# Pooled attention and two MLPs on one core: a scheduler that hands out PSUM banks when they come free, an earlier release of a conversion's source block, and other DMA costs

## The chip, the core and the metric

The kernel runs on one core of a Trainium2 chip. The metric is the device time of one execution in microseconds (us). Five engines work side by side, each through its own queue in order: TensorE (PE, matmuls into the eight PSUM banks), ScalarE (ACT), VectorE (DVE), GpSimd (POOL) and SyncE (SP, which issues all DMAs here).

## The reference

```python
q_pool = q.reshape(B, H, S // 2, 2, D).mean(axis=3)          # 4 batches, 8 heads, 1152 rows, 64 wide
scores = (1 / sqrt(D)) * q_pool @ k.T                         # 576 x 1152 a head
attn   = exp(scores - max) / (sum(exp) + 1e-9)
x = (attn @ v) as [2304 tokens, 512]
h = x @ moe_w_in;  x = max(0.01 * h, h) @ moe_w_out           # 512 -> 2048 -> 512
h = x @ moe2_w_in; out = where(h > 0, h, exp(min(h, 0)) - 1) @ moe2_w_out
```

The four weight matrices reach the kernel as float64, and the kernel turns their bits into float32 itself. Each float32 operand is split in a high and a low part in a rounded format, and products take two or three matmuls.

## The kernel before

Work is recorded as operations with an engine, a cost in ns, a rank and a function; `Program.schedule` then plays a clock forward and starts, on each idle engine, the open operation of least rank, and `emit` writes the instructions in the order of the starts. What the engines run is that order, each in its own queue; on the chip an instruction waits only for its data and its buffers. So costs, latencies and buffer rules in the scheduler move instructions and change none.

There are 16 attention pairs (four batches, four pairs of heads) of nine score tiles each. A score tile is three blocks of 384 keys, each a PSUM bank: matmuls (L486), a maximum on DVE (L491), the exponential on ACT (L497), transposes (L509) of its result into PSUM, a high part on ACT and a low part on DVE (L298, L304), then the product with v (L530). Beside the attention of batches 1 to 3 run the two MLPs of the batch before; those of batch 3 come last and alone ("wide"). An MLP has 16 steps; in each, 24 matmuls (L672) fill two banks, ACT and DVE empty them (L683, L685 in the first MLP; L688, L691, L693 in the second), and after each four steps `down` forms eight more banks (L710), which ACT or DVE adds up (L720, L723). `store` transposes the result (L744), copies it on ACT into one of two `cr` buffers (L750) and sends it out.

PSUM before: tags with a fixed number of banks, taken in turn in the order in which operations were recorded: `s` 3 for scores, `t` 2 for transposes, `o` 1 for the product with v, `h` 2 for the MLPs. In the first four pairs transposes also take `h` banks; a wide MLP takes `h`, `t` and `s` banks in turn.

`convert` fetches a block of float64 into `cr` (L327, two buffers), reads its high words on ACT into `cm` (L330), its low words on ACT in place (L332), shifts on DVE (L334) into `ct`, adds on POOL (L337) reading `cr`, and merges on DVE into the weight tile `wr` (L339). Each block is converted once, stored to DRAM and read back for the later batches.

An operation of class `Port` is a DVE operation that shares SBUF ports with POOL by the scheduler's account; it never plays one beside a POOL operation. POOL gives way to an open `Port` operation that DVE will soon be free for (`HOLD` 500 ns) if that one's rank is below POOL's rank plus `HELD`.

Of the kernel before, what the change touches and what calls it, by code (L numbers as in the profile page):

```python
# [22 lines left out]
class Buf:  # L23


    def __init__(self, make, prev=None, before=None):
        self.make, self.prev, self.before = make, prev, before
        self.tile, self.first = None, None
        self.writers, self.readers = [], []

# [3 lines left out]
    @property  # L34
    def ap(self):
        if self.tile is None:
            self.tile = self.make()
        return self.tile


class Program:

# [7 lines left out]
    HELD = 5  # L50
    LATENCY = {"PE": 200, "SP": 2500, "DVE": 130, "DVE POOL": 200, "ACT": 155, "ACT POOL": 170, "POOL": 150,
               "PE PE": 5}

    def __init__(self):
        self.ops, self.tags = [], {}
# [7 lines left out]
    def add(self, engine, cost, rank, fn, w=(), r=()):  # L63

        me = len(self.ops)
        deps, starts, frees = set(), set(), []
# [8 lines left out]
        for x in w:  # L75
            b, part = x if isinstance(x, tuple) else (x, None)
            deps.update(hits(b.writers, part))
            deps.update(hits(b.readers, part))
            if b.first is None:
                b.first = me  # L80
            if b.prev is not None:
# [5 lines left out]
        self.ops.append((engine, cost, rank, fn, deps, starts, frees))  # L87

    def schedule(self):
# [3 lines left out]
        for i, (_, _, _, _, deps, starts, frees) in enumerate(ops):  # L93
# [9 lines left out]
            need[i] = len(d | starts)  # L103
        ready = [0.0] * n
# [10 lines left out]
        left = n  # L115
        while left:
# [4 lines left out]
            while again:  # L121
                again = False
                for e in sorted(idle, key=lambda e: e == "POOL"):
# [5 lines left out]
                    i = open_[e][0][1]  # L129
                    if e == "POOL":  # L130
                        if port > now:
                            continue
                        if idle["DVE"] <= now + self.HOLD and any(
                                isinstance(ops[o][1], Port) and r < ops[i][2] + self.HELD
                                for r, o in open_["DVE"]):
                            if idle["DVE"] > now:
                                heapq.heappush(times, idle["DVE"])
                                continue
                    if e == "DVE" and port > now and isinstance(ops[i][1], Port):
                        others = [x for x in open_[e] if not isinstance(ops[x[1]][1], Port)]  # L140
                        if not others:
                            continue
                        x = min(others)
                        open_[e].remove(x)
                        heapq.heapify(open_[e])
                        heapq.heappush(open_[e], (-1e9, x[1]))
                        i = x[1]
# [4 lines left out]
                    heapq.heappop(open_[e])  # L152
# [4 lines left out]
                    if e == "POOL" or isinstance(ops[i][1], Port):  # L157
                        port = end
                    again = True
                    for o, done in out[i]:  # L160
                        e2 = ops[o][0]
                        if not done:
                            t = now
                        elif e2 == "PE" and e not in ("PE", "SP"):
                            t = end + 200
                        else:
                            t = end + self.LATENCY.get(e + " " + e2, self.LATENCY[e])
                        ready[o] = max(ready[o], t)
                        need[o] -= 1
                        if not need[o]:  # L170
                            heapq.heappush(waiting[e2], (ready[o], o))
                            heapq.heappush(times, ready[o])
        return start

    def emit(self, tc):
        start = self.schedule()
        held, name = None, None
        for i in sorted(range(len(start)), key=lambda i: (start[i], i)):
            engine, cost, _, fn, deps, _, _ = self.ops[i]
# [11 lines left out]
def kernel(  # L191
# [54 lines left out]
    SBUFS = 3  # L246
    RAWB = 3
    EARLY = {'s': 'sss', 't': 'tthh'}
    T1B = 3
    HBUFS = 2  # L250
# [3 lines left out]
    TB = 2  # L254
# [27 lines left out]
    def bank(tag, shape, dt=F32, bufs=1):  # L282
        return prog.buf(tag, bufs, lambda: ps.tile(shape, dt, tag=tag, name=tag, bufs=bufs))
# [8 lines left out]
    def pool(n):  # L292
        return 140 + 2.12 * n

    def psplit(rank, h, l, hi, lo, src, n, w, r, w_l=None, fast=True, psum=False):
# [3 lines left out]
        else:  # L299
            prog.add("DVE", dve(n, fast), rank, lambda: V.tensor_copy(out=hi(), in_=src()), w=[w], r=r)  # L300
# [7 lines left out]
    def convert(rank, dst, src):  # L308

        for n in range(0, 512, CW):
            r = sb("cr", [128, CW, 2], U32, CB)
            t = sb("ct", [128, CW], U32, CB)
            g = sb("cm", [128, CW], F32, CB)

            def load(n=n, r=r):  # L320
# [8 lines left out]
            prog.add("SP", 60, rank - 1, load, w=[r])  # L329
            prog.add("ACT", act(CW, sbuf=True), rank, lambda r=r, g=g: A.activation(  # L330
                out=g.ap, in_=r[:, :, 1].bitcast(F32), func=ACTF.Copy, scale=REBIAS), w=[g], r=[(r, 1)])
            prog.add("ACT", act(CW, sbuf=True), rank, lambda r=r: A.activation(  # L332
                out=r[:, :, 0], in_=r[:, :, 0], func=ACTF.Copy, scale=2.0 ** -29), w=[(r, 0)], r=[(r, 0)])
            prog.add("DVE", dve(CW, True), rank, lambda g=g, t=t: V.tensor_scalar(  # L334
                out=t.ap, in0=g.ap.bitcast(U32), scalar1=3, scalar2=None,
                op0=ALU.logical_shift_left), w=[t], r=[g])
            prog.add("POOL", pool(CW), rank, lambda t=t, r=r: G.tensor_tensor(  # L337
                out=t.ap, in0=t.ap, in1=r[:, :, 0], op=ALU.add), w=[t], r=[t, (r, 0)])
            prog.add("DVE", dve(CW, port=True), rank, lambda n=n, t=t, g=g: V.scalar_tensor_tensor(  # L339
                out=dst[:, n:n + CW].bitcast(U32), in0=g.ap.bitcast(U32), scalar=0x80000000, in1=t.ap,  # L340
                op0=ALU.bitwise_and, op1=ALU.bitwise_or), w=[(dst, n)], r=[t, g])
# [3 lines left out]
    def load_w(rank, layer, w_in, w_out, f, mine):  # L345
# [4 lines left out]
        for i, r in enumerate(rs):  # L350
            if w_in.dtype == F32:
                view = (lambda r=r: r.ap.rearrange("p (c n) -> p c n", c=DC)) if i == 0 else lambda r=r: r.ap
                prog.add("SP", 60, rank - 1.5, lambda i=i, view=view: nc.sync.dma_start(
                    out=view(), in_=src[i]), w=[r])
            elif (layer, f, i) in kept:
                kp = kept[layer, f, i]
                prog.add("SP", 60, rank - 1.5, lambda r=r, kp=kp: nc.sync.dma_start(
                    out=r.ap, in_=kp.ap), w=[r], r=[kp])
            else:
                convert(rank - CLEAD, r, src[i])  # L360
                kp = kept[layer, f, i] = Buf(lambda i=i: dram.tile([128, 512], F32, name=f"w{layer}_{f}_{i}"))
                prog.add("SP", 60, rank, lambda r=r, kp=kp: nc.sync.dma_start(out=kp.ap, in_=r.ap), w=[kp], r=[r])
# [17 lines left out]
    def load(rank, key, tag, shape, pieces, bufs):  # L380
        t = sb(tag, shape, F32, bufs)
        for i, (to, src) in enumerate(pieces):
            prog.add("SP", 60, rank, lambda to=to, src=src: nc.sync.dma_start(out=to(t), in_=src), w=[(t, i)])
# [18 lines left out]
    def tr_r(rank, src, get, n):  # L402
# [6 lines left out]
        prog.add("PE", 70 * n, rank, go, w=[t], r=[src])  # L409
        return t  # L410

    def prep_k(rank, b, hp, j):
# [5 lines left out]
        for c in range(3):  # L418
            t = tr_r(rank, kn, lambda i, c=c: kn[:, 3 * c + i, :], 3)
# [18 lines left out]
    def prep_q(rank, b, hp, j):  # L438
        qn = q_split(rank, raw[b, hp, j, "q"], QT, "q")
        qT = sb("qT", [128, 2, QT, 128], F32R, KTB)  # L440
        for a in range(2):
            t = tr_r(rank, (qn, a), lambda i, a=a: qn[:, a, i, :], QT)
# [4 lines left out]
    def prep_rem(rank, b, hp):  # L447
        qn = q_split(rank, raw[b, hp, "x"], 1, "qx")
        t = tr_r(rank, qn, lambda i: qn[:, i, 0, :], 2)
# [13 lines left out]
    turns = {}  # L463
    BANKS = dict(s=SBUFS, t=TB, o=1, h=HBUFS)

    def pbank(use, dt=F32, shape=(128, 4, 128)):
        tags = (EARLY if first_window[0] else {}).get(use, use)
        n = turns[use] = turns.get(use, -1) + 1
        tag = tags[n % len(tags)]
        return bank(tag, list(shape), dt, BANKS[tag])  # L470
# [32 lines left out]
    def transpose_p(rank, p, dests):  # L503
        for c in ORDER:
# [8 lines left out]
            prog.add("PE", 3 * 108, rank, tr, w=[t], r=[(p, c)])  # L513
# [9 lines left out]
    def pv(rank, b, hp, j, pt, col0, n):  # L523
        o = pbank("o", F32, (128, 512))
        vn = prep[b, hp, j, "v"]

# [7 lines left out]
        for th in ORDER:  # L534
            prog.add("PE", 6 * (7 + 0.4375 * n), rank + PVLAG, lambda th=th: mm(th), w=[o], r=[vn, pt[th]])
        if (b, hp) not in xu:
            xu[b, hp] = sb("xu", [128, NQ], F32, XFB)
        x = xu[b, hp]
        hi, lo = slice(64 * j, 64 * j + 64), slice(64 - 64 * j, 128 - 64 * j)
        tm = sb("tm", [128, 5 * 64])  # L540
        prog.add("ACT", act(n), rank + PVLAG, lambda: A.activation(
# [87 lines left out]
    def mlp(at, span, b, layer, xin, w_in, w_out, tags):  # L629

        step = span / (FT + 1)
        turn = [0]

        def hbank():
            tag, bufs = tags[turn[0] % len(tags)]
            turn[0] += 1
            return bank(tag, [128, 512], F32, bufs)
# [3 lines left out]
        def mine(tag, shape, dt, bufs, other, more):  # L641

            seq = ((tag, bufs),) * bufs + (((other, more),) * more if len(tags) > HBUFS else ())
# [17 lines left out]
        def up(f):  # L661
# [4 lines left out]
            for hf in range(2):  # L666
                cols = slice(hf * HB, hf * HB + HB)
                h = hbank()

# [10 lines left out]
                t = mine("t1", [128, HB], F32, T1B, "raw", RAWB)  # L680
# [52 lines left out]
    def store(at, b, acc, tags):  # L733
        turn = 0
        for t in range(QT + 1):
            n = 128 if t < QT else RQ
            tag, bufs = tags[turn % len(tags)]
            turn += 1
            p = bank(tag, [128, 512], F32, bufs)
# [15 lines left out]
            prog.add("SP", 60, at, lambda o=o, n=n, rows=rows: nc.sync.dma_start(  # L755
# [56 lines left out]
```

## Time and profile before

| | |
|---|---|
| median of 3 runs | 1486.04 us (1485.85 to 1488.83) |
| the profiled execution | 1488.3 us, span 1486.5 us |
| PE busy | 1403.5 us, 94% of the span |
| ACT busy | 1058.6 us, 71% |
| DVE busy | 886.0 us, 60% |
| POOL busy | 811.7 us, 55% |
| DMA | 135.6 MB, 91 GB/s |

Busy time is the time in which an engine has an instruction under way. Instructions of one engine overlap, and the ends of matmuls are modelled, so the spacing of starts tells more than the busy share. An idle time of PE under 150 ns is not listed as a wait.

### The profile page before, as it was taken

What the parts mean: (1) busy time and instruction counts of PE and PEld (TensorE: products, weight loads), DVE (VectorE), ACT (ScalarE), POOL (GpSimd) and SP (SyncE); (2) the same over time, 40 slices, a digit from 0 to 9 for tenths busy, and PEclk for the clock granted to TensorE, in tenths of its full rate; (3) what the DMA queues carried; (4) which work ended last, traced back from release to release, by engine and by line L of the source; (5) the groups of instructions that cost most, each with busy time, mean ns of one, the idle gap of its engine ahead of it and who ended that gap; (6) DMA issues with size and microseconds to landing.
All of it is one profiled execution on the core that took longest, in us unless ns stands there. A gap on an engine that the chain in (4) does not pass through costs nothing.

```text
span 1486.5 us, 28829 instructions
## 1 busy us (share of the span) xinstructions
PE 1403.5 (94%) x10288; PEld 1357.7 (91%) x10288; DVE 886.0 (60%) x2145; ACT 1058.6 (71%) x2901; POOL 811.7 (55%) x840
## 2 busy tenths in 40 slices
PE   6888899999998899999999999999999999899998
PEld 5777798898988888899999999999999999899998
DVE  5888787787867676456575656556575553124222
ACT  7999889788888877677667677776667764542643
POOL 5454355667667666454554456554454445666661
PEclk9999999999999999999999999999999999999999
DMA  4233224334443443322221222321221222322210
GB/s 136 97 104 105 62 74 154 122 125 136 142 132 130 140 157 115 102 83 66 73 61 60 68 80 73 112 67 59 73 67 43 58 72 64 118 85 79 72 51 33
DMA packets 82641, 135.58 MB, mean 91 GB/s; under 512 B 8512, under 2 KB 26944, under 8 KB 82496
## 3 DMA queue, kind: packets, MB, share of 16 engines
q1 hardware_dynamic: 82496, 133.73, 28.8%
q8 instruction: 81, 1.33, 0.4%
q14 instruction: 64, 0.52, 0.1%
HBM read 112.20 MB, written 21.50 MB: 90 GB/s over the span
## 4 chain that ended last, share of the span: by engine, by line
PE 54%; ACT 3%; DVE 1%; DMA 1%; POOL 1%; issue 1%; ACTq 0%; DVEq 0%; POOLq 0%
PE h L710 16%; PE h L672 14%; PE s L486 5%; PE o L530 5%; PE t L509 4%; PE s L672 3%; PE s L710 2%; PE t L672 2%; PE t L710 2%; PE t L407 1%; DMA out_dram<-cr 1%; ACT t L688 1%; DVE t L693 1%; ACT t L691 0%; ACT wi L298 0%
## 5 line engine op out<-in xcount | busy, mean ns | idle before, releaser
L710 PE MATMUL h<-g,wo 128*128 128x288 f32 x2460 | 425.8, 302 | 2.8 <-DVE t L693 1.8
L672 PE MATMUL h<-xs,wi 128*128 128x288 f32 x2448 | 414.2, 304 | 14.6 <-ACT cr L750 6.5
L672 PEld LDWEIGHTS h<-xs,wi 128*128 128x128 f32 x2448 | 350.2, 190 | 22.2 <-DVE t L693 7.7
L710 PEld LDWEIGHTS h<-g,wo 128*128 128x128 f32 x2460 | 354.8, 188 | 6.1 <-DVE t L693 3.4
L491 DVE TENSOR_REDUCE m<-s 128x1 f32<-128x384 f32 x432 | 230.4, 551 | 75.3 <-PE s L486 71.8
L298 ACT ACTIVATE pt<-t 128x384 fp32r<-128x384 f32 (+2 forms) x426 | 190.4, 458 | 108.7 <-PE t L509 102.0
L304 DVE TENSOR_TENSOR pt<-t,pt 128x384 fp32r<-128x384 f32 (+1 forms) x416 | 207.8, 510 | 87.3 <-ACT pt L298 85.5
L497 ACT ACTIVATE p<-s,m 128x384 f32<-128x384 f32 x432 | 251.0, 592 | 9.1 <-DVE m L493 8.7
L304 POOL TENSOR_TENSOR g<-t,g 128x288 fp32r<-128x288 f32 x216 | 174.4, 813 | 97.0 <-ACT g L298 63.6
L486 PE MATMUL s<-kT,qT 128*128 128x384 f32 x768 | 194.7, 356 | 30.6 <-ACT p L497 30.2
L530 PE MATMUL o<-pt,vn 128*128 128x256 f32 (+1 forms) x1152 | 189.5, 301 | 1.5 <-DVE pt L304 1.0
L509 PE MATMUL t<-ident,p 128*128 128x128 f32 x1116 | 181.6, 275 | 4.9 <-DVE pt L304 2.4
L304 POOL TENSOR_TENSOR wo<-wr,wo 128x512 fp32r<-128x512 f32 x112 | 144.4, 1295 | 72.8 <-ACT wo L298 58.5
L304 POOL TENSOR_TENSOR wi<-wr,wi 128x512 fp32r<-128x512 f32 x110 | 142.3, 1294 | 64.1 <-ACT wi L298 18.8
L530 PEld LDWEIGHTS o<-pt,vn 128*128 128x128 f32 x1152 | 165.6, 190 | 4.2 <-DVE pt L304 3.9
L486 PEld LDWEIGHTS s<-kT,qT 128*128 128x128 f32 x768 | 124.5, 191 | 44.0 <-ACT p L497 41.8
L509 PEld LDWEIGHTS t<-ident,p 128*128 128x128 f32 x1116 | 137.9, 141 | 13.4 <-DVE pt L304 3.7
L304 POOL TENSOR_TENSOR vn<-raw,vn 128x576 fp32r<-128x576 f32 x32 | 45.7, 1427 | 166.5 <-ACT vn L298 135.4
L337 POOL TENSOR_TENSOR ct<-ct,cr 128x256 uint32<-128x256 uint32 x128 | 94.5, 747 | 68.1 <-DVE ct L334 14.4
L723 DVE TENSOR_TENSOR acc<-h,acc 128x288 f32<-128x288 f32 x158 | 71.1, 453 | 66.5 <-PE h L710 63.9
L298 ACT ACTIVATE g<-t 128x288 fp32r<-128x288 f32 x216 | 96.6, 452 | 13.6 <-DVE t L693 8.1
L298 ACT ACTIVATE wo<-wr 128x512 fp32r<-128x512 f32 x112 | 70.7, 635 | 38.5 <-PE h L710 31.7
(149 smaller groups left out, 2081.8 us busy)
## 6 DMA issues: line engine op xcount, KB each, us to landing
wr<-w SPq DMA_DIRECT2D x172, 256.0 KB, 2.7
cr<-in_moe_w_in_dram SPq DMA_DIRECT2D x64, 256.0 KB, 2.9
cr<-in_moe_w_out_dram SPq DMA_DIRECT2D x64, 256.0 KB, 2.8
w<-wr SPq DMA_DIRECT2D x64, 256.0 KB, 3.1
raw<-in_k_dram SPq DMA_DIRECT2D x32, 288.0 KB, 3.0
raw<-in_v_dram SPq DMA_DIRECT2D x32, 288.0 KB, 3.0
raw<-in_q_dram SPq DMA_DIRECT2D x32, 256.0 KB, 2.7
p<-w SPq DMA_DIRECT2D x20, 256.0 KB, 2.6
```

Of the source, the lines that this page charges most:

```text
L298: prog.add("ACT", act(n, sbuf=not psum), rank, lambda: A.activation(out=hi(), in_=src(), func=ACTF.Copy), w=[w], r=r)
L304: lambda: eng.tensor_tensor(out=lo(), in0=src(), in1=f32(hi()), op=ALU.subtract),
L337: prog.add("POOL", pool(CW), rank, lambda t=t, r=r: G.tensor_tensor(out=t.ap, in0=t.ap, in1=r[:, :, 0], op=ALU.add), w=[t], r=[t, (r, 0)])
L407: PE.transpose(out=t[:, i, :], in_=get(i), identity=identr)
L486: PE.matmul(out=st[:, 0:384], lhsT=qa(a), rhs=kT[:, 384 * c:384 * c + 384], start=(i == 0), stop=(i == len(seq) - 1))
L491: prog.add("DVE", dve(384), rank - LR, lambda st=st, c=c: V.tensor_reduce(out=m[:, c:c + 1], in_=st[:, 0:384], axis=AX.X, op=ALU.max), w=[ ...
L497: prog.add("ACT", act(384, True), rank - LE, lambda c=c: A.activation(out=p[:, 384 * c:384 * c + 384], in_=banks[c][:, 0:384], func=ACTF.E ...
L509: PE.transpose(out=t[:, i, :], in_=p[:, (3 * c + i) * 128:(3 * c + i + 1) * 128], identity=ident)
L530: PE.matmul(out=o[:, 0:n], lhsT=vn[:, c, :], rhs=pt[th][:, a, c % 3, :], start=(c == 3 * ORDER[0] and a == 0), stop=(c == 3 * ORDER[2] + 2 ...
L672: PE.matmul(out=h[:, 0:HB], lhsT=wi[:, a, c, :], rhs=xs[c][:, e, cols], start=(c == 0 and a == 0 and e == 0), stop=(c == DC - 1 and a == 1))
L710: PE.matmul(out=y[:, 0:HB], lhsT=w[f][1][:, a, d * 128:(d + 1) * 128], rhs=g[f][:, e, cols], start=(f % FC == 0 and a == 0 and e == 0), st ...
L723: prog.add("DVE", dve(HB), rank - HURRY, lambda y=y, a_=a_, cols=cols: V.tensor_tensor(out=a_[:, cols], in0=y[:, 0:HB], in1=a_[:, cols], o ...
```

## The change

- **Banks.** All eight banks are one pool. A use (`s`, `t`, `o`, `h`) has a cap on banks held at once, `CAPS`, one set for the first four pairs, one for the middle and one for a wide MLP. When the scheduler starts an operation that opens a bank, it takes the bank that came free first in its clock; if none is free or the cap is met, it tries the engine's other open operations by rank. `want` makes a PE operation also wait, in the scheduler, until the SBUF buffer that its result will go to is free; `down`'s first operation of a bank also waits for all four steps' activations.
- **Conversion.** The low words go to `ct` and not back into `cr`, so `cr` is read by the two ACT steps alone; the shift, the add and the merge now all write the weight tile.
- **Numbers.** A DMA costs 400 ns of SP and 2600 ns to land (before 60 and 2500); some ACT and POOL costs grow by 16 to 80 ns; `HELD` is 0 (before 5).

The number of instructions on each engine is the same before and after, and so is their work.

```diff
-    HELD = 5
-    LATENCY = {"PE": 200, "SP": 2500, ...
+    HELD = 0
+    BANKS = 8
+    LATENCY = {"PE": 200, "SP": 2600, ...
...
+        def can(i, now):
+            if port > now and (ops[i][0] == "POOL" or isinstance(ops[i][1], Port)):
+                return False
+            if ops[i][7]:
...
+                if any(held.get(u, 0) + k > dict((b.use, b.cap) for b in ops[i][7])[u] for u, k in count.items()):
+                    return False
+                if sum(t <= now for t, _ in free) < len(ops[i][7]):
+                    return False
+            return True
...
+                    x = open_[e][0]
+                    if not can(x[1], now):
+                        if e == "POOL":
                             continue
...
+                        x = next((y for y in sorted(open_[e]) if can(y[1], now)), None)
...
+                    for b in ops[i][7]:
+                        t, k = min(free)
+                        free.remove((t, k))
+                        b.bank = k
...
-    SBUFS = 3
-    EARLY = {'s': 'sss', 't': 'tthh'}
-    HBUFS = 2
-    TB = 2
+    CAPS = (dict(s=4, t=4, o=1, h=2), dict(s=3, t=2, o=1, h=3), dict(s=3, t=2, o=1, h=7))
...
-            prog.add("SP", 60, rank - 1, load, w=[r])
-            prog.add("ACT", act(CW, sbuf=True), rank, lambda r=r: A.activation(
-                out=r[:, :, 0], in_=r[:, :, 0], func=ACTF.Copy, scale=2.0 ** -29), w=[(r, 0)], r=[(r, 0)])
...
-            prog.add("POOL", pool(CW), rank, lambda t=t, r=r: G.tensor_tensor(
-                out=t.ap, in0=t.ap, in1=r[:, :, 0], op=ALU.add), w=[t], r=[t, (r, 0)])
+            prog.add("SP", 400, rank - 1, load, w=[r])
...
+            prog.add("ACT", act(CW, sbuf=True) + 20, rank, lambda r=r, t=t: A.activation(
+                out=t.ap, in_=r[:, :, 0], func=ACTF.Copy, scale=2.0 ** -29), w=[t], r=[r])
...
+            prog.add("POOL", pool(CW), rank, lambda t=t, to=to: G.tensor_tensor(
+                out=to(), in0=to(), in1=t.ap, op=ALU.add), w=part, r=[t] + part)
...
-                             w=[h], r=[wi, (xs[c], hf), (xs[c], 2 + hf)])
+                             w=[h], r=[wi, (xs[c], hf), (xs[c], 2 + hf)], want=[g[f], t])
```

Three places in the instruction order show what moves. `h_`, `s_`, `t_`, `o_` name a PSUM tile by its old tag, `b0_` to `b7_` a PSUM tile by its bank.

PE near the end of the second MLP of batch 2, where no attention is left beside it; before:

```order
L672 MATMUL h_17617<-xs_15767,wi_17305 128x288 x3
L672 MATMUL h_17641<-xs_15644,wi_17380 128x288 x3
L672 MATMUL h_17641<-xs_15666,wi_17380 128x288 x3
L672 MATMUL h_17641<-xs_15731,wi_17380 128x288 x3
L672 MATMUL h_17641<-xs_15767,wi_17380 128x288 x3
L672 MATMUL h_17665<-xs_15644,wi_17380 128x288 x3
L672 MATMUL h_17665<-xs_15666,wi_17380 128x288 x3
L672 MATMUL h_17665<-xs_15731,wi_17380 128x288 x3
L672 MATMUL h_17665<-xs_15767,wi_17380 128x288 x3
L672 MATMUL h_17690<-xs_15644,wi_17602 128x288 x3
```

The same place after:

```order
L737 MATMUL b3_17528<-g_17137,wo_16722 128x288 x3
L700 MATMUL b4_17629<-xs_15667,wi_17319 128x288 x3
L737 MATMUL b3_17528<-g_17233,wo_17075 128x288 x3
L700 MATMUL b4_17629<-xs_15674,wi_17319 128x288 x3
L700 MATMUL b2_17648<-xs_15667,wi_17319 128x288 x3
L700 MATMUL b4_17629<-xs_15740,wi_17319 128x288 x3
L700 MATMUL b2_17648<-xs_15674,wi_17319 128x288 x3
L700 MATMUL b4_17629<-xs_15772,wi_17319 128x288 x3
L700 MATMUL b2_17648<-xs_15740,wi_17319 128x288 x3
L737 MATMUL b3_17528<-g_17294,wo_17152 128x288 x3
L700 MATMUL b2_17648<-xs_15772,wi_17319 128x288 x3
L700 MATMUL b0_17682<-xs_15667,wi_17383 128x288 x3
```

Before, `h_17690` takes the bank of `h_17641` again with the 12 matmuls of one other group between. After, groups of `down` stand between those of the MLP's first half, several banks are open at once, and bank 4 is not opened again before 27 more rows.

PE where the third pair of batch 0 ends and the fourth begins, with attention alone; before:

```order
L486 MATMUL s_2044<-kT_1923,qT_1987 128x384 x2
L509 MATMUL t_2049<-ident_58,p_2040 128x128 x3
L486 MATMUL s_2056<-kT_1923,qT_1987 128x384 x2
L509 MATMUL t_2060<-ident_58,p_2040 128x128 x3
L486 MATMUL s_2068<-kT_1923,qT_1987 128x384 x2
L509 MATMUL h_2073<-ident_58,p_2040 128x128 x3
L530 MATMUL o_2083<-pt_2023,vn_1480 128x256 x6
L530 MATMUL o_2083<-pt_2030,vn_1480 128x256 x6
L530 MATMUL o_2083<-pt_2033,vn_1480 128x256 x6
L486 MATMUL s_2122<-kT_1923,qT_1987 128x384 x2
```

The same part after:

```order
L444 MATMUL b6_2053<-identr_63,kn_1844 128x128 x3
L444 MATMUL b7_2063<-identr_63,kn_1844 128x128 x3
L444 MATMUL b6_2070<-identr_63,kn_1844 128x128 x3
L444 MATMUL b1_2075<-identr_63,qn_1882 128x128 x4
L444 MATMUL b0_2085<-identr_63,qn_1882 128x128 x4
L517 MATMUL b7_2093<-kT_1780,qT_1824 128x384 x2
L540 MATMUL b6_2099<-ident_58,p_2013 128x128 x3
L517 MATMUL b1_2108<-kT_1780,qT_1824 128x384 x2
L540 MATMUL b5_2114<-ident_58,p_2013 128x128 x3
L540 MATMUL b0_2120<-ident_58,p_2013 128x128 x3
L517 MATMUL b6_2131<-kT_1780,qT_1824 128x384 x2
```

Before, `s_2122` takes the bank of `s_2044` again, 31 matmuls later. After, scores and transposes share banks: bank 6 goes from keys to keys with three matmuls between, then to a transpose and, eight matmuls later, to scores.

ACT in a conversion beside the attention of batch 1; before:

```order
L298 ACTIVATE kn_3473<-raw_2981 128x9x64
L330 ACTIVATE cm_3487<-cr_3426 128x256
L332 ACTIVATE cr_3426<-cr_3426 128x256
L330 ACTIVATE cm_3494<-cr_3443 128x256
L332 ACTIVATE cr_3443<-cr_3443 128x256
L443 ACTIVATE qT_3502<-t_3468 128x512
```

The same step after:

```order
L748 ACTIVATE acc_3454<-b5_3355 128x288
L367 ACTIVATE cm_3460<-cr_3386 128x256
L369 ACTIVATE ct_3462<-cr_3386 128x256
L367 ACTIVATE cm_3467<-cr_3392 128x256
L369 ACTIVATE ct_3477<-cr_3392 128x256
L480 ACTIVATE qT_3427<-b0_3415 128x512
```

The second step of each block writes `ct` where it wrote `cr`; the two blocks stand behind each other as before, among other neighbours.

## Rows read from the trace of the kernel before

**Rows 1.** Page, part 1: busy time, share of the span, instructions.

```profile
PE 1403.5 (94%) x10288; PEld 1357.7 (91%) x10288; DVE 886.0 (60%) x2145; ACT 1058.6 (71%) x2901; POOL 811.7 (55%) x840
```

**Rows 2.** Windows (PE, PEld, DVE, ACT, POOL busy us and instructions; clock; DMA).

```profile
50.00:100.00 50.00, 42.04 (x296) 37.62 (x295) 42.84 (x113) 49.03 (x142) 25.38 (x26) 1.00 0.30 98
700.00:750.00 50.00, 50.00 (x385) 49.82 (x384) 30.05 (x69) 31.19 (x83) 30.03 (x31) 1.00 0.29 82
...
0.00:200.00 200.00, 162.75 (x1114) 146.45 (x1115) 159.88 (x418) 176.82 (x507) 84.23 (x96) 0.99 0.31 95
200.00:600.00 400.00, 370.02 (x2668) 352.83 (x2666) 296.43 (x728) 326.86 (x921) 261.25 (x287) 0.99 0.42 134
600.00:1200.00 600.00, 598.06 (x4495) 590.55 (x4496) 345.88 (x809) 422.16 (x1146) 304.70 (x297) 1.00 0.23 70
1200.00:1487.00 287.00, 272.63 (x2017) 267.82 (x2015) 83.84 (x193) 132.73 (x329) 161.53 (x161) 0.99 0.24 73
```

**Rows 3.** Waits of PE: who for whom, total us, times, longest; 0 to 195 us.

```profile
PE s L486 <- ACT p L497: 23.1, 22, 2.3
```

**Rows 4.** Waits of all engines, 195 to 600 us.

```profile
ACT cm L330 <- DMA cr<-in_moe_w_out_dram: 16.9, 16, 1.8
ACT cm L330 <- DMA cr<-in_moe_w_in_dram: 16.7, 22, 2.1
PE s L486 <- ACT p L497: 11.2, 14, 2.1
```

**Rows 5.** Waits of PE for an emptied MLP bank, 195 to 600 us, then from 1200 us.

```profile
PE h L672 <- DVE t L693: 2.3, 4, 1.3
...
PE h L710 <- DVE acc L723: 0.2, 1, 0.2
...
PE h L672 <- ACT cr L750: 3.6, 1, 3.6
PE h L710 <- DVE t L693: 1.1, 3, 0.8
```

**Rows 6.** Groups by line and shape: count, busy us, mean ns, idle before.

```profile
L298 ACT ACTIVATE pt<-t 128x384 fp32r<-128x384 f32 x328 | 158.5, 492 | 83.6 <-PE t L509 82.7
L304 DVE TENSOR_TENSOR pt<-t,pt 128x384 fp32r<-128x384 f32 x328 | 178.5, 553 | 68.1 <-ACT pt L298 66.7
L683 ACT ACTIVATE t<-h 128x288 f32<-128x288 f32 x105 | 43.9, 419 | 31.2 <-PE h L672 26.8 <-POOL g L304 2.6 <-POOL ct L337 1.5
L685 DVE TENSOR_TENSOR t<-h,t 128x288 f32<-128x288 f32 x105 | 47.5, 453 | 79.7 <-ACT t L683 79.0
```

**Rows 7.** Timeline of PE about the third store (start, us, instruction, idle before).

```profile
1271.60 1.11 PE L744 MATMUL h<-ident,acc 128*128 128x128 f32 x8
1276.27 4.96 PE L672 MATMUL h<-xs,wi 128*128 128x288 f32 x24 [3.55 <-ACT cr L750]
```

**Rows 8.** Windows there, columns as above.

```profile
1276.00:1280.00 4.00, 3.73 (x16) 3.73 (x17) 0.00 (x0) 0.81 (x2) 0.84 (x1) 0.57 0.53 164
1280.00:1284.00 4.00, 3.74 (x29) 3.51 (x28) 1.37 (x3) 3.09 (x10) 1.85 (x3) 1.00 0.00 0
```

**Rows 9.** Chain of waits about the first store, 575 to 606 us.

```profile
587.83 0.40 PE h L710 x3
```

**Rows 10.** DMA issues by SP: count, ns min/median/max; then KB and us to landing.

```profile
L327 SPq DMA_DIRECT2D cr<-in_moe_w_in_dram x64: 378/379/1248, 4.6 to 550.2; - x64
...
cr<-in_moe_w_in_dram SPq DMA_DIRECT2D x64, 256.0 KB, 2.9
```

**Rows 11.** DVE operations of the port class: ns min/median/max, and means by group.

```profile
L334 DVE TENSOR_SCALAR ct<-cm x128: 229/293/1035, 8.1 to 560.0; 128x256 uint32<-128x256 uint32 x128
L339 DVE SCALAR_TENSOR_TENSOR wr<-cm,ct x128: 365/417/1505, 23.8 to 564.8; 128x256 uint32<-128x256 uint32 x128
...
L339 DVE SCALAR_TENSOR_TENSOR wr<-cm,ct 128x256 uint32<-128x256 uint32 x128 | 67.3, 540 | 6.8 <-POOL ct L337 6.4
L334 DVE TENSOR_SCALAR ct<-cm 128x256 uint32<-128x256 uint32 x128 | 47.2, 372 | 22.3 <-ACT cm L330 21.2
```

More of the change, by code (lines that the diff above doesn't have):

```diff
@@ L61, in buf, with bank, add @@
         return b
-    def add(self, engine, cost, rank, fn, w=(), r=()):
+    def bank(self, use, cap, make):
+        b = Buf(make, use=use)
+        b.cap = cap
+        self.psum.append(b)
+        return b
+    def add(self, engine, cost, rank, fn, w=(), r=(), want=()):
         me = len(self.ops)
-        deps, starts, frees = set(), set(), []
+        deps, starts, frees, allocs = set(), set(), [b.prev for b in want if b.prev is not None], []
         def hits(accesses, part):
@@ L103, in schedule @@
             need[i] = len(d | starts)
+        uses = [[] for _ in range(n)]
+        left_in = {}
+        for b in self.psum:
+            users = {o for o, _ in b.writers + b.readers}
+            left_in[b] = len(users)
+            for o in users:
+                uses[o].append(b)
+        free = [(0.0, k) for k in range(self.BANKS)]
+        last = [None] * self.BANKS
+        held = {}
+        self.after = {}
         ready = [0.0] * n
@@ L128, in schedule @@
                         continue
[L129 to L131 removed]
+                    x = open_[e][0]
+                    if not can(x[1], now):
+                        if e == "POOL":
                             continue
[L133 to L141, printed above, removed]
[L142 to L147 removed]
+                        x = next((y for y in sorted(open_[e]) if can(y[1], now)), None)
+                        if x is None:
+                            continue
+                    i = x[1]
+                    if e == "POOL" and idle["DVE"] <= now + self.HOLD and idle["DVE"] > now and any(
+                            isinstance(ops[o][1], Port) and r < ops[i][2] + self.HELD for r, o in open_["DVE"]):
+                        continue
                     if e != "SP" and any(
@@ L158, in schedule @@
                         port = end
+                    for b in ops[i][7]:
+                        t, k = min(free)
+                        free.remove((t, k))
+                        b.bank = k
+                        held[b.use] = held.get(b.use, 0) + 1
+                        if last[k] is not None:
+                            self.after.setdefault(i, set()).update(
+                                o for o, _ in last[k].writers + last[k].readers)
+                        last[k] = b
+                        b.until = 0.0
+                    for b in uses[i]:
+                        b.until = max(b.until, end + self.latency(e, "PE"))
+                        left_in[b] -= 1
+                        if not left_in[b]:
+                            free.append((b.until, b.bank))
+                            held[b.use] -= 1
+                            heapq.heappush(times, b.until)
                     again = True
@@ L161, in schedule @@
                         e2 = ops[o][0]
[L162 to L167, printed above, removed]
+                        t = end + self.latency(e, e2) if done else now
                         ready[o] = max(ready[o], t)
@@ L299, in psplit @@
         else:
-            prog.add("DVE", dve(n, fast), rank, lambda: V.tensor_copy(out=hi(), in_=src()), w=[w], r=r)
+            prog.add(h, dve(n, fast) if h == "DVE" else pool(n), rank,
+                     lambda: (V if h == "DVE" else G).tensor_copy(out=hi(), in_=src()), w=[w], r=r)
         eng = V if l == "DVE" else G
```

122 lines of the change are left out of this document (62 added, 60 removed).

## Prediction

> **What bounds the kernel now.** I read the page's busy shares first. PE is under way for 1403.5 us of 1486.5 [rows 1]; ACT comes next with 71%. So PE is the engine to count, but a busy PE is not a full one. The window from 700 to 750 us gives the spacing of a full PE: 385 matmuls in 50 us with no idle time, 0.130 us each [rows 2]. 10288 of them are 1337 us, so some 149 us of the span are lost, nearly twice the 83 us that the busy time leaves. By stage, with the counts of [rows 2]: 0 to 200 us, 1114 x 0.130 = 145, lost 55; 200 to 600, 2668 x 0.130 = 347, lost 53; 600 to 1200, 4495 x 0.130 = 584, lost 16; from 1200, where nearly all are MLP matmuls of 0.133 us (three in 0.40, [rows 9]), 2017 x 0.133 = 268, lost 18. These add to 142; the rest is the mix of shapes.
>
> The stages have different limits. From 0 to 200 us attention runs alone: PE waits 22 times, 23.1 us in all, for an exponential to free a score bank [rows 3], while ACT is under way 49.03 of 50 us [rows 2]. ACT and the bank cycle share that stage. From 200 to 600 us no engine is full (PE 370 of 400, ACT 327, DVE 296, POOL 261); ACT's queue stands 38 times, 33.6 us, for a float64 block to land, and PE 14 times, 11.2 us, for an exponential [rows 4]. From 600 to 1200 us PE is under way 598 of 600 us: there the kernel is near what PE can do. After 1200 us PE runs MLP alone and waits for banks [rows 5, 7].
>
> For the rule on reading this: the Trainium skill (Perfetto Trace Analysis, "Identifying the Most-Contended Engine") calls matmul busy time a poor measure of headroom and takes the busy share of weight loads in its place. Here weight loads leave 1486.5 - 1357.7 = 129 us [rows 1]. The trace sides with it: the spacing's 149 us lies nearer to 129 than to 83. If only 83 us were to be had and the same quarter of them came back, the gain would be some 21 us and the time 1467.
>
> **The change part by part.** No instruction is added or removed; matmul work stays 1337 us. What can change is the 149 us.
>
> *Banks in the MLPs.* Emptying a bank takes an ACT step and a DVE step that both read it, 419 + 453 = 872 ns plus two hand-offs [rows 6]; I take 1.2 us, nine matmuls. With two `h` banks a bank is written again after one other group: counted over PE's order from the 600 us mark to the 1200 us mark, the median distance behind a bank of `down` is 14 matmuls, and 40 of 112 have fewer than 12; after the change 21, and 8 of 112. From 1200 us on: 12 before, 34 of 77 under 12; after, 75 and none. A wait of this kind that shows is up to 1.3 us long [rows 5], and many are hidden inside modelled ends. From 600 to 1200 us I take back 4 of the 16 us (bounds 0 and 12). After 1200 us the largest piece is one store: ACT's copy waits for an earlier one to leave `cr`, both `h` banks are held, PE idles 3.55 us, and the next 24 matmuls take 4.96 us where 24 x 0.133 = 3.2 would do [rows 7], 1.8 us more. The granted clock says why: 0.57 over the 4 us after the pause, so partly at the lower level of 1.2 GHz, and 1.00 again in the next 4 [rows 8]. With up to seven banks, groups behind the store find another: 3.55 + 1.8 = 5.3, and 2.7 of the other waits there, 8 in all (bounds 0 and 13; the last store's copy and DMA stay). The order's piece near 1240 us shows it: 12 matmuls between two uses of a bank before, 27 rows after.
>
> *Banks in the first stage.* Scores gain a fourth bank, and the median distance behind a score bank grows from 25 to 37 matmuls. Transposes pay: 21 falls to 11, and 56 of 110 have fewer than 12 where 8 of 111 had. A transposed bank is emptied by ACT in 492 and DVE in 553 ns [rows 6], 1.05 us, eight matmuls, plus hand-offs: just covered at 11, not at the 6 of the lowest tenth. ACT leaves 200 - 177 = 23 us at most. Bounds: 23 us gained, or 56 x 0.5 = 28 lost. I take 6 gained, a quarter of the 23.1 that PE waits for score banks, since ACT remains nearly full.
>
> *The middle stage: conversion and DMAs.* `cr` was held until POOL had added; it is now free after two ACT steps, so a load can be issued earlier. The scheduler planned 60 ns and 2500 ns for a load; the trace shows 378 ns of SP and 2.9 us to land [rows 10], and it now plans 400 and 2600. ACT steps should stand where their block has landed, and the 33.6 us of ACT's queue should mostly go. ACT is busy four fifths of this stage and PE waits for it only at times: I count a quarter, 9 us. Of the waits for exponentials, 11.2, and for MLP banks, 5.7 over seven pairs of waiter and cause (2.3 the largest, 0.2 the least, [rows 5]), two thirds go with the pool: 11. Together 20 of the 53 us (bounds 0 and 45). The weight tile `wr` is held through shift, add and merge rather than the merge alone, longer by the shift's 372 ns [rows 11] and POOL's add, so by some 1 us with hand-offs. Thirty-two steps share 400 us, 12.5 us a step; a step takes two of four `wr`, so each has 25 us, and I count nothing. Without that cover it would be 32 x 1 = 32 us.
>
> *`HELD` and the costs* only move instructions; their price is in the rivals.
>
> Sum: 6 + 20 + 4 + 8 = 38 us. The profiled execution took 1488.3 us, 1.8 more than its span, so 1450.3; the median of the runs shown is 2.3 us lower, which puts the forecast at 1449 beside 1486.04.
>
> **The rivals.**
>
> *ACT and DVE hold the first 600 us.* Shorter bank waits then only turn into waits for the same exponentials: the first term is 0, the middle keeps 6, the other two stay: 18 us, 1470. For it: ACT at 49 of 50 us from 50 to 100 us. Against: from 200 us on it is at 82%.
>
> *Transposes starve in the first stage.* The 28 us of the bound come, and one more bank is lost, since in the new order the first MLP bank is opened beside the third pair and closed only after the fourth. The other terms give 32, so 1488.3 - 32 + 28 = 1484. For it: 56 short distances. Against: PE has idle time there, so that eleven matmuls last longer than 1.4 us.
>
> *Slower: POOL holds DVE.* With `HELD` at 0 POOL gives way only to DVE operations of lower rank than its own. A merge takes 365 ns at best, 540 on average, 1505 at worst; a shift 229, 372, 1035 [rows 11]. The excess over the best is 128 x (0.175 + 0.143) = 41 us of DVE already, and casts of the same class add some 15. DVE runs in order, so maxima and low parts of the attention stand behind a held operation. If the 56 us double and all of it lies on the path, the first two terms go and the time is 1488.3 - 12 + 56 = 1532; with half of it on the path, 1504, which is what I take. It decides once more than 38 us of new blocking reach PE. Against: a POOL operation still gives way where the DVE operation is the more urgent by rank, and before it yielded only five ranks more. The Trainium skill (SBUF — State Buffer, "Who interferes with whom") has the mechanism: the first to issue gets the shared port pair for its whole instruction and the other blocks fully. The worst merge above, 1505 ns against 365, agrees.
>
> *The change does nothing.* On the chip a bank is free when its reader is done, whatever the scheduler planned; if its clock is off by a microsecond, first-free in the plan is not first-free in fact: 1486.
>
> **How the numbers follow.** The forecast has 0.50, with a range of its own from 1425 to 1465; ACT and DVE as the limit 0.20; starved transposes 0.10; POOL holding DVE 0.12; nothing 0.05; and 0.03 for a gain near the upper bounds, 23 + 45 + 12 + 13 = 93, below 1416. Half of the transposes' case and all but the slow case and "nothing" are faster by over 0.2%, 3 us, about what a measurement of this kernel can tell: 0.50 + 0.20 + 0.03 + 0.05 = 0.78. Within 0.2%: 0.08. Slower: 0.14. The range from 1416 to 1487 leaves out 0.14 above and 0.03 below.
>
> **What would show it.** Right: in the first 200 us the waits of PE's score matmuls fall from 23.1 us, with some new waits of transposes; from 200 to 600 us ACT's waits for `cr` fall well under 33.6 us and PE works off more than 2668 matmuls; from 600 to 1200 us little changes; the pause of 3.55 us and the low clock after it are gone. Wrong: merges and shifts with means above 540 and 372 ns; waits of PE for transposed banks above 20 us in the first stage; or the same waits for exponentials under new bank names, with a span within 3 us of before.

## The result: 43 us faster, 3% less

The kernel after takes 1443.89 us (median of 4 runs, 1442.06 to 1445.43) beside 1487.43 us for the kernel before on the same chip; the ratio is 0.9698, 95% interval 0.9665 to 0.9732. The forecast was 1449, its range 1416 to 1487. The profiled span is 1443.1 us.

Page of the kernel after, part 1, columns as in [rows 1]:

```profile
PE 1395.5 (97%) x10288; PEld 1356.8 (94%) x10288; DVE 884.7 (61%) x2145; ACT 1057.3 (73%) x2901; POOL 811.6 (56%) x840
```

The same instructions run about as long as before (PE is under way 8 us less, the other engines at most 1.3); it is the span that is shorter. Windows of the kernel after, columns as in [rows 2]:

```profile
0.00:200.00 200.00, 176.47 (x1180) 153.51 (x1181) 167.95 (x434) 182.44 (x530) 90.24 (x103) 0.99 0.31 98
200.00:600.00 400.00, 392.71 (x2922) 382.68 (x2921) 314.61 (x758) 347.36 (x980) 278.11 (x304) 1.00 0.44 141
600.00:1200.00 600.00, 595.61 (x4481) 591.51 (x4480) 334.06 (x806) 414.40 (x1134) 301.50 (x294) 0.99 0.23 69
```

From 200 to 600 us PE starts 2922 matmuls where it started 2668: 254 more, 33 us at 0.130 us. From 600 to 1200 us it starts 14 fewer. The two largest waits of score matmuls in the kernel after, 0 to 195 us:

```profile
PE b L517 <- DVE pt L344: 4.1, 9, 0.8
...
PE b L517 <- ACT p L528: 1.1, 2, 0.9
```

The 23.1 us of [rows 3] are 1.1; what scores now wait for, 4.1 us, is a transposed bank that DVE has yet to empty. From 195 to 600 us ACT waits 5.7 us for float64 blocks, in four rows, where it waited 33.6 us by [rows 4] and 35.2 with two smaller rows. The largest of the four stands below. Above it stands a wait that is new: ACT's second step now writes `ct`, and the two `ct` buffers are held until POOL has added.

```profile
ACT ct L369 <- POOL wr L374: 8.7, 16, 2.1
...
ACT cm L367 <- DMA cr<-in_moe_w_out_dram: 2.3, 1, 2.3
```

To compare stages whose boundaries move, I sum the matmuls in order at their median spacing in the kernel before (1345 us in all) and note how far the clock is ahead of this sum: the time that PE has lost by then. The stretches are cut at 140 us of work (batch 0's attention), 560 (about the end of the conversions) and 1120 (the last attention).

| lost by PE, us | to 140 | 140 to 560 | 560 to 1120 | rest | all |
|---|---|---|---|---|---|
| before | 58.4 | 54.3 | 11.4 | 11.1 | 135.2 |
| after | 49.5 | 19.3 | 13.0 | 9.8 | 91.6 |
| gain | 8.9 | 35.0 | -1.6 | 1.3 | 43.6 |

### The profile page after: what moved, and what is told of

The parts are those of the page before. It is cut to its first block, busy times and chain, and to the rows that moved or that the text cites. A ratio compares the mean times of both kernels' runs of the same rounds, so it can differ in the third digit from the quotient of the medians.

```text
span 1443.1 us, 28887 instructions
## 1 busy us (share of the span) xinstructions
PE 1395.5 (97%) x10288; PEld 1356.8 (94%) x10288; DVE 884.7 (61%) x2145; ACT 1057.3 (73%) x2901; POOL 811.6 (56%) x840
## 4 chain that ended last, share of the span: by engine, by line
PE 72%; ACT 14%; DVE 8%; DMA 2%; issue 2%; POOL 2%; ACTq 0%; SPq 0%; POOLq 0%; DVEq 0%
PE b L737 24%; PE b L700 23%; PE b L517 8%; PE b L564 8%; PE b L540 6%; ACT p L528 3%; ACT pt L337 2%; PE b L444 2%; DVE pt L344 2%; DVE m L522 2%; ACT cm L367 1%; DMA cr<-in_moe_w_in_dram 1%; ACT ct L369 1%; ACT g L337 1%; DMA cr<-in_moe_w_out_dram 1%
## 5 line engine op out<-in xcount | busy, mean ns | idle before, releaser
L737 PE MATMUL b<-g,wo 128*128 128x288 f32 x2784 | 497.3, 302 | 3.2 <-POOL g L344 1.9
L700 PE MATMUL b<-xs,wi 128*128 128x288 f32 x2784 | 477.8, 302 | 6.1 <-POOL xs L344 2.2
L700 PEld LDWEIGHTS b<-xs,wi 128*128 128x128 f32 x2784 | 403.1, 190 | 10.9 <-POOL xs L344 3.1
L737 PEld LDWEIGHTS b<-g,wo 128*128 128x128 f32 x2784 | 407.5, 189 | 4.5 <-POOL g L344 2.2
L344 DVE TENSOR_TENSOR pt<-b,pt 128x384 fp32r<-128x384 f32 (+1 forms) x480 | 235.8, 512 | 66.6 <-ACT pt L337 64.0
L337 ACT ACTIVATE pt<-b 128x384 fp32r<-128x384 f32 (+1 forms) x480 | 209.9, 470 | 88.4 <-PE b L540 85.8
L522 DVE TENSOR_REDUCE m<-b 128x1 f32<-128x384 f32 x432 | 231.1, 551 | 65.0 <-PE b L517 62.5
L528 ACT ACTIVATE p<-b,m 128x384 f32<-128x384 f32 x432 | 252.6, 600 | 3.9 <-DVE m L524 3.7
L540 PE MATMUL b<-ident,p 128*128 128x128 f32 x1296 | 207.1, 275 | 6.7 <-DVE pt L344 1.6
L564 PE MATMUL b<-pt,vn 128*128 128x256 f32 (+1 forms) x1152 | 191.5, 300 | 6.5 <-ACT pt L337 3.5
L540 PEld LDWEIGHTS b<-ident,p 128*128 128x128 f32 x1296 | 159.2, 141 | 19.1 <-DVE pt L344 3.9
```

What stands on the lines that cost most here:

```text
L337: prog.add("ACT", act(n, sbuf=not psum), rank, lambda: A.activation(out=hi(), in_=src(), func=ACTF.Copy), w=[w], r=r)
L344: lambda: eng.tensor_tensor(out=lo(), in0=src(), in1=f32(hi()), op=ALU.subtract),
L522: prog.add("DVE", dve(384), rank - LR, lambda st=st, c=c: V.tensor_reduce(out=m[:, c:c + 1], in_=st[:, 0:384], axis=AX.X, op=ALU.max), w=[ ...
L528: prog.add("ACT", act(384, True), rank - LE, lambda c=c: A.activation(out=p[:, 384 * c:384 * c + 384], in_=banks[c][:, 0:384], func=ACTF.E ...
L540: PE.transpose(out=t[:, i, :], in_=p[:, (3 * c + i) * 128:(3 * c + i + 1) * 128], identity=ident)
L564: PE.matmul(out=o[:, 0:n], lhsT=vn[:, c, :], rhs=pt[th][:, a, c % 3, :], start=(c == 3 * ORDER[0] and a == 0), stop=(c == 3 * ORDER[2] + 2 ...
```

## Experiments

Each is timed beside the kernel before on its chip (1488.4 to 1488.8 us there), so the ratios compare better than the times. Lost time is from the one profiled execution, which took 1487.4 us for e4 and 1451.9 for e9, 6 and 4 us above their medians.

| run | what | us | ratio (95%) | to 140 | 140 to 560 | 560 to 1120 | rest |
|---|---|---|---|---|---|---|---|
| e1 | before + conversion | 1482.6 | 0.9959 (0.9944, 0.9975) | 63.4 | 44.2 | 11.4 | 11.0 |
| e2 | before + DMA costs | 1476.3 | 0.9928 (0.9904, 0.9953) | 57.1 | 37.8 | 15.0 | 10.8 |
| e3 | before + both | 1473.0 | 0.9903 (0.9882, 0.9925) | 62.2 | 32.2 | 13.9 | 11.8 |
| e4 | after - both | 1481.8 | 0.9952 (0.993, 0.9975) | 57.5 | 50.7 | 13.4 | 12.5 |
| e5 | after - DMA costs | 1462.2 | 0.9824 (0.9799, 0.9848) | 54.6 | 31.0 | 11.6 | 12.6 |
| e6 | after - conversion | 1455.2 | 0.9784 (0.9758, 0.981) | 46.5 | 34.2 | 11.4 | 8.4 |
| e7 | after, ACT latency 157 | 1444.5 | 0.9706 (0.9684, 0.9728) | 48.2 | 19.9 | 11.4 | 11.2 |
| e8 | after, two MLP banks | 1440.8 | 0.9681 (0.966, 0.9702) | 49.9 | 22.8 | 4.0 | 11.2 |
| e9 | after, last-freed bank | 1447.8 | 0.9735 (0.9716, 0.9754) | 49.2 | 21.8 | 17.2 | 9.8 |
| e10 | after, HELD 2 | 1449.0 | 0.9734 (0.9717, 0.9751) | 48.4 | 25.4 | 11.5 | 10.7 |
| e11 | e8, DMA lands after 2900 | 1443.7 | 0.9698 (0.9679, 0.9717) | 48.5 | 25.6 | 5.4 | 11.6 |
| e12 | e8, casts on POOL | 1435.6 | 0.9645 (0.9629, 0.9662) | 45.6 | 24.1 | 3.5 | 9.7 |

**e1, the conversion alone.**

```diff
-    out=r[:, :, 0], in_=r[:, :, 0], func=ACTF.Copy, scale=2.0 ** -29), w=[(r, 0)], r=[(r, 0)])
+    out=t.ap, in_=r[:, :, 0], func=ACTF.Copy, scale=2.0 ** -29), w=[t], r=[r])
```

> The kernel before, with the new conversion alone (low words go to ct, cr is free after two ACT steps); banks, DMA costs and HELD as before. Theory A (the pool of banks made most of the 43 us): at most 8 us faster, 1479 to 1490. Theory B (ACT queueing for float64 blocks made the middle stage slow): ACT's waits for cr between 195 and 600 us fall from 33.6 us to under 20, and the time to 1466 to 1478.

**e2, the DMA costs alone.**

```diff
-    prog.add("SP", 60, ...          "SP": 2500
+    prog.add("SP", 400, ...         "SP": 2600
```

The costs change at all six places that issue a DMA.

> The kernel before, with the new DMA costs alone (400 and 2600 ns in the scheduler). Theory A: within 8 us of before, 1479 to 1492. Theory B: ACT steps are placed where their block has landed, waits for cr fall to under 20 us and the time to 1466 to 1478.

**e3, both edits above.**

> The kernel before, with the new conversion and the new DMA costs, and banks by tag as before. Theory A: 1475 to 1488, the waits of PE for score banks in the first 195 us stay near 23 us. Theory B: waits for cr under 8 us, time 1455 to 1470, about half of the 43 us or more.

**e4, the kernel after with both edits undone.**

> The kernel after, with the conversion and the DMA costs of before: the pool of banks, want and HELD 0 stay. Theory A: 1445 to 1457, 30 us or more of the 43 are kept. Theory B: 1460 to 1475, and ACT's waits for cr between 195 and 600 us stay above 25 us.

Neither theory holds. By its time e1 lies in A's range and e2 in B's, e3 between the two and e4 outside both. The pool without the two edits gives 7 us, against the 30 that A wanted; conversion and DMA costs together give 15, below B's half. Besides the pool, e4 has `want`, `HELD` 0 and the changed costs of ACT and POOL; a pool with the old `HELD` of 5 was not run. Waits from 195 to 600 us, in e4, in e2 and in e1:

```profile
ACT cm L366 <- DMA cr<-in_moe_w_in_dram: 19.3, 24, 2.2
...
ACT cm L366 <- DMA cr<-in_moe_w_out_dram: 9.3, 12, 1.9
```

```profile
ACT cm L330 <- DMA cr<-in_moe_w_out_dram: 10.3, 18, 1.4
...
ACT cm L330 <- DMA cr<-in_moe_w_in_dram: 10.0, 14, 1.2
```

```profile
ACT ct L334 <- POOL wr L339: 17.0, 25, 2.6
...
ACT ct L334 <- DMA cr<-in_moe_w_in_dram: 7.6, 8, 1.8
```

The new conversion takes most of the wait for `cr` away, but part of it comes back as the wait for `ct`. All rows of the two kinds, 195 to 600 us, beside what PE loses in the middle stage:

| us | ACT waits for `cr` | its `ct` step for POOL | both | lost, 140 to 560 | lost less waits |
|---|---|---|---|---|---|
| before | 35.2 | - | 35.2 | 54.3 | 19.1 |
| e1 | 9.5 | 17.0 | 26.5 | 44.2 | 17.7 |
| e2 | 20.3 | - | 20.3 | 37.8 | 17.5 |
| e3 | 1.3 | 9.9 | 11.2 | 32.2 | 21.0 |
| e4 | 29.2 | - | 29.2 | 50.7 | 21.5 |
| e5 | 8.3 | 12.5 | 20.8 | 31.0 | 10.2 |
| e6 | 14.6 | - | 14.6 | 34.2 | 19.6 |
| after | 5.7 | 8.7 | 14.4 | 19.3 | 4.9 |

With banks by tag (before, e1 to e3) a microsecond of these waits goes with about one of PE's. That is agreement over four runs and no proof, as the DMA costs move other loads too. With the pool as well the last column falls, but only where the new conversion is in.

The gains do not add: 6 + 12 + 7 = 25 us of 43.5. The 7 is the least sure of them. The ten runs of e4 go from 1474.1 us, at a mean granted clock of 0.994, to 1487.4 at 0.986. That last one was profiled, and its windows show the clock at 0.97 and 0.98 where [rows 2] have 0.99:

```profile
0.00:200.00 200.00, 170.88 (x1118) 148.12 (x1119) 161.89 (x418) 176.49 (x509) 87.04 (x98) 0.97 0.31 96
200.00:600.00 400.00, 373.68 (x2685) 359.15 (x2684) 297.10 (x724) 326.03 (x915) 262.59 (x291) 0.98 0.42 133
```

The two mean clocks differ by 0.008, 12 us over the span, by estimate. So e4's lost times are partly the clock's, and why it falls more often there is not shown. At 1474.1 the pool's gain would be 14 us and the sum 32, still short of 43.5.

**e5, the kernel after with the old DMA costs, and e6, with the old conversion.**

```diff
-    prog.add("SP", 400, ...         "SP": 2600
+    prog.add("SP", 60, ...          "SP": 2500
```

> The kernel after with the DMA costs of before (60 and 2500 ns in the scheduler). Theory C (the pool pays only where the planned landing of a float64 block is right, since a late block stops ACT's queue while banks are held): 1462 to 1475, ACT's waits for cr between 195 and 600 us above 15 us, lost time of PE in the middle stage 35 us or more. Theory D (each part adds its own few us, so the joint gain is an accident of the order): 1470 to 1478, the sum of the separate gains.

> The kernel after with the conversion of before, so that cr is held until POOL has added. Theory C: 1448 to 1460, most of the gain stays, since planned times are right; ACT's waits for cr stay under 12 us. Theory D: 1466 to 1475.

Both times lie inside C's ranges, e5 by 0.2 us, and outside D's: either edit on top of the pool gives 20 to 27 us, where alone it gave 6 or 12. C's account is half wrong, though. In e6 ACT waits 14.6 us for `cr`, not under 12. In e5 it waits 8.3 us, not over 15 (7.0 of them in the two ACT rows below, 195 to 600 us), and the middle stage loses 31.0 us, not 35:

```profile
POOL qs L468 <- DMA raw<-in_q_dram: 6.6, 2, 6.0
...
ACT ct L369 <- DMA cr<-in_moe_w_out_dram: 4.5, 8, 1.2
...
ACT ct L369 <- DMA cr<-in_moe_w_in_dram: 2.5, 6, 0.9
```

So waits for float64 blocks do not account for what the DMA costs give e5 to become the kernel after (18 us, 11.7 of it in the middle stage). Other loads, of keys, queries, values and weights, are planned with the same numbers; which of them it is was not tried, nor the 400 apart from the 2600. The trace has one candidate: POOL stands 6.6 us for loads of queries in e5 and 1.1 in the kernel after, but it stands 4.3 in e12, which takes least time of all.

**e7, an idle change of a number.**

```diff
-    LATENCY = {... "ACT": 155, ...
+    LATENCY = {... "ACT": 157, ...
```

> The kernel after with ACT's latency in the scheduler at 157 instead of 155 ns: another order of much of PE's work (1779 lines of difference) with no reason to be better or worse. It measures how far the order's accidents alone move the time. Theory C: within 6 us of the kernel after, 1438 to 1450. Theory D: anywhere from 1440 to 1465.

0.6 us from the kernel after. This one other order changes little beside the differences above, but the 3 to 5 us of the runs below rest on medians of four executions that spread over 2 to 5 us.

**e8, two MLP banks beside attention.**

```diff
-    CAPS = (dict(s=4, t=4, o=1, h=2), dict(s=3, t=2, o=1, h=3), ...
+    CAPS = (dict(s=4, t=4, o=1, h=2), dict(s=3, t=2, o=1, h=2), ...
```

> The kernel after with two banks at most for the MLPs beside attention (cap h of 2 instead of 3), still out of the pool. If the third bank made the pool's gain between 200 and 1200 us: 4 to 15 us slower than after, 1448 to 1459, with waits of MLP matmuls for DVE back. If taking the bank that came free first made it: within 4 us of after.

It is 3 us faster, so the third bank is not what helps; with two, taken anywhere in the pool, few are opened again early (8 of 111 of `down`'s with fewer than 12 matmuls between, from 600 to 1200 us, the same as with three). What it gains, 13.0 to 4.0 us lost between 560 and 1120, is mostly two pauses near 728 and 1072 us of the kernel after: in e8 PE waits for no `pt` of ACT between 560 and 1200 us. The first reads, in PE's timeline and then in ACT's:

```profile
727.60 1.18 PE L540 MATMUL b<-ident,p 128*128 128x128 f32 x6
730.55 1.69 PE L564 MATMUL b<-pt,vn 128*128 128x320 f32 x6 [1.77 <-ACT pt L337]
```

```profile
724.82 0.63 ACT L337 ACTIVATE wo<-wr 128x512 fp32r<-128x512 f32 x1 [2.73 <-DMA wr<-w]
726.57 0.71 ACT L715 ACTIVATE t<-b 128x288 f32<-128x288 f32 x2 [1.12 <-PE b L700]
...
729.65 0.63 ACT L337 ACTIVATE wi<-wr 128x512 fp32r<-128x512 f32 x1
730.17 0.33 ACT L337 ACTIVATE pt<-b 128x192 fp32r<-128x192 f32 x1
```

ACT stands 2.73 us for a weight load and soon after 1.12 us for an MLP bank that PE is filling. From 726.57 us it works without a pause, and the part of `pt` that PE wants comes behind activations and weight casts in its queue. How much of this the late load makes is not shown.

**e9, the bank that came free last.**

```diff
-                        t, k = min(free)
+                        t, k = max(f for f in free if f[0] <= now)
```

> The kernel after with the same instruction order on every engine, but each new bank is the one that came free last in the scheduler's clock and not first. Banks of down that are opened again with fewer than 12 matmuls between grow from 12 to 32 (of 63) beside batch 1 and from 8 to 60 (of 112) beside batches 2 and 3. Theory C1 (the slack of the first-freed bank is what the pool gives): 8 to 25 us slower than after, 1452 to 1469, PE waiting for DVE and ACT at MLP banks again. Theory C2 (the order, with any free bank taken by whoever can start, is what it gives): within 5 us of after.

4 us above the median of the kernel after: inside C2's range, below C1's, and not clear of noise, since the intervals of the two ratios overlap. PE's waits after 195 us are of the kind that C1 expected: 3.1 and 2.8 us, the latter a single wait, where the kernel after has 0.8 and 0.5.

```profile
PE b L700 <- DVE t L720: 3.1, 5, 1.3
PE b L737 <- DVE t L720: 2.8, 1, 2.8
```

So the slack of the first-freed bank is worth some 4 us at most; the rest of the gain stays with the same order of instructions.

**e10, POOL gives way a little more.**

```diff
-    HELD = 0
+    HELD = 2
```

> The kernel after with HELD at 2 instead of 0, so that POOL gives way to more DVE operations. The rival of the prediction (POOL holds DVE): 5 to 15 us faster than after, and the mean of the conversion's merge falls. The other reading (it is one more accident of the order): within 5 us of after, like the run with ACT's latency at 157.

5 us slower than the kernel after, where the rival asked for 5 to 15 faster, so the rival falls. Groups of the conversion on DVE (mean ns), in the kernel after and in e10:

```profile
L376 DVE SCALAR_TENSOR_TENSOR wr<-cm,wr 128x256 uint32<-128x256 uint32 x128 | 68.2, 553 | 5.0 <-POOL wr L374 4.5
...
L371 DVE TENSOR_SCALAR wr<-cm 128x256 uint32<-128x256 uint32 x128 | 53.9, 438 | 5.1 <-ACT cm L367 4.7
```

```profile
L376 DVE SCALAR_TENSOR_TENSOR wr<-cm,wr 128x256 uint32<-128x256 uint32 x128 | 69.6, 564 | 5.2 <-POOL wr L374 4.5
...
L371 DVE TENSOR_SCALAR wr<-cm 128x256 uint32<-128x256 uint32 x128 | 52.9, 431 | 7.6 <-ACT cm L367 7.4
```

Giving way more does not shorten the merge, and the shift by only 7 ns.

**e11, a later planned landing, on e8.**

```diff
-    "SP": 2600
+    "SP": 2900
```

> The kernel of the run with two MLP banks beside attention (e8), with a DMA planned to land after 2900 instead of 2600 ns. If a late block is still what costs in the middle stage, 2 to 6 us faster than e8, 1435 to 1439. If the plan is now true enough, within 3 us of e8.

3 us slower than e8, at the edge of what was said for a plan that is true enough: a later plan gives nothing.

**e12, casts of the first stage on POOL, on e8.**

```diff
-        psplit(rank, KH, "POOL", lambda: kn[:, :, 0:D], ...
+        psplit(rank, "POOL" if first_window[0] and (b, hp) != pairs[0] else KH, "POOL", lambda: kn[:, :, 0:D], ...
```

The same edit stands at `vn`.

> The kernel of e8, with the high parts of keys and values of the first four pairs (but the first pair's) made on POOL instead of ACT: about 14 steps, 0.58 us each, 8 us less on ACT and 20 us more on POOL in the first stage. If ACT sets the first stage: 3 to 8 us faster than e8, 1433 to 1438. If the chain through banks, DVE and POOL sets it: no change or some us slower, as POOL then makes both parts of a key in turn.

5 us faster than e8, 4.3 of them before 140 us of work: 49.9 lost become 45.6. Windows of e8, then of e12:

```profile
0.00:200.00 200.00, 175.16 (x1174) 151.95 (x1175) 166.39 (x433) 181.47 (x528) 88.00 (x100) 1.00 0.31 98
```

```profile
0.00:200.00 200.00, 177.24 (x1207) 156.46 (x1207) 169.57 (x444) 178.72 (x525) 99.36 (x117) 1.00 0.31 99
```

So ACT limits that stage, at least in part: POOL does more, ACT less, and PE starts 33 matmuls more. With 1435.6 us this is the fastest version run, 8 us under the kernel after by medians.

## Why the prediction was right, and where its sum was off

*The reading of the loss* was right, and where it lies. The 149 us by one spacing are 142 by each shape's own (1345 us of work), 6 of them behind the last matmul. The kernel got back 43.5 us; the idle time by the busy share fell only from 83 to 48.

*First stage, 6 us:* 8.9 measured. The waits for exponentials went from 23.1 to 1.1 us, and transposes wait a little, as forecast. But that is not yet the gain. In e4 these waits are as short, from 0 to 195 us, and PE still loses 57.5 us of 58.4 (the clock's 0.97 against 0.99 is some 4 us of 200, by estimate):

```profile
PE b L516 <- ACT p L527: 1.3, 2, 1.1
```

With the new DMA costs on top (e6) the loss is 46.5, with the new conversion (e5) 54.6. So the fourth score bank pays here mainly together with the DMA costs, which the sum had in the middle stage alone. ACT stayed a limit, as e12 shows.

*Middle stage, 20 us:* 35.0 measured; this is the term that was mis-sized, by its first part. I gave the conversion and the DMA costs 9 us, a quarter of ACT's waits, since PE waits for ACT only at times. In e3, which has them without the pool, ACT's waits fall by 24 us and PE loses 22 less between 140 and 560 us of work: nearly one for one. The reading that fits is that in a queue in order ACT's pause delays all that stands behind it, PE's operands among it. I also took the wait as gone once `cr` is free early; e1 shows half of it again, for `ct`. The pool's 11 us came out as 13 (32.2 to 19.3) on top of e3, but as 4 without it (e4, with its low clock). That the parts need each other was not in the sum at all.

*600 to 1200 us, 4 us:* -1.6. MLP waits went, and two pauses came in which PE waits for ACT (e8).

*After 1200 us, 8 us:* 1.3. The store's pause of 3.55 us is gone as forecast, since PE finds other banks; others take its place. Timeline of PE in the kernel after, where the last batch's MLP begins:

```profile
1209.83 0.94 PE L737 MATMUL b<-g,wo 128*128 128x288 f32 x5 [1.92 <-POOL g L344]
1210.61 0.29 PE L700 MATMUL b<-xs,wi 128*128 128x288 f32 x1
1213.07 0.85 PE L700 MATMUL b<-xs,wi 128*128 128x288 f32 x2 [2.17 <-POOL xs L344]
1213.72 0.92 PE L737 MATMUL b<-g,wo 128*128 128x288 f32 x3
```

The chain there goes over DVE's casts of the new input:

```profile
1206.03 2.08 DVE xs L340 x4
...
1209.21 1.39 DVE xs L340 x4
...
1212.23 0.80 POOL xs L344
```

So the sum came within 5 us of the median partly by luck: the middle got 15 us too little and the first stage 3, the other two 12 too much. There is also a slip in it: 1450.3 less 2.3 is 1448.0, not 1449. My reason for the MLP banks, the number of banks, fell (e8); the distance between uses, which the count gave, holds in sign and is worth 4 us at most (e9).

*The rivals.* Starved transposes: PE's waits for them in the first stage are far below 20 us. POOL holding DVE: one sign of being wrong did show, merges at 553 ns beside 540 and shifts at 438 beside 372 on average, but DVE's busy time did not grow, the span fell, and e10 speaks against it. ACT and DVE as the limit was half true: ACT still limits the first stage, yet 8.9 us came there where that rival had none.

## What to carry to other kernels

Where a scheduler writes the order, check its costs for what is off the bottleneck first. A load was planned for 60 + 2500 ns where the trace had 378 ns and 2.9 us [rows 10]; an instruction that waits for such a load at the head of its queue holds everything behind it. Freeing one buffer early can move a wait to the next one: follow it (`cr` to `ct`). Test edits together as well as apart: the pool with what comes with it gave 7 us alone, about 20 beside either of the other edits (e1 to e5, e2 to e6) and 29 beside both (e3 to the kernel after). Look at the granted clock before reading a difference of a few us, as in e4. Count loss by the spacing of starts and by work done, since the busy share hid nearly half of it.

## What the runs showed of the hardware

After a pause of 1.77 us PE's granted clock fell. Windows of the kernel after about 728 us; the value behind POOL's is the granted clock:

```profile
724.00:728.00 4.00, 3.97 (x29) 3.58 (x27) 0.70 (x2) 2.06 (x6) 2.36 (x2) 1.00 0.23 81
728.00:731.00 3.00, 1.08 (x6) 0.55 (x5) 1.35 (x4) 2.91 (x9) 2.10 (x3) 1.00 0.27 87
731.00:735.00 4.00, 4.00 (x18) 4.00 (x19) 0.92 (x2) 1.16 (x3) 3.91 (x4) 0.57 0.35 82
735.00:739.00 4.00, 4.00 (x33) 4.00 (x32) 1.35 (x4) 2.65 (x9) 0.33 (x1) 1.00 0.36 114
```

18 matmuls start in 4 us at 0.57, for the most part at 1.2 GHz, and 33 in the next four at 2.4 GHz: 15 fewer at 0.130 us, so the slow clock after the pause cost about as much as the pause. The length of a pause does not decide it alone: in the kernel before PE stood 1.98 us for a score bank, and the clock of 50 to 100 us stayed at 1.00 [rows 2].

```profile
89.39 0.62 PE L486 MATMUL s<-kT,qT 128*128 128x384 f32 x2 [1.98 <-ACT p L497]
```
